# Local attention with global tokens, fused with a SoLU feed-forward: PSUM in two shared pools, q and k loaded 8 tokens a partition, and dummy products on the tensor engine

## The chip, the cores and the metric

The kernel runs on 1 core of one Trainium2 chip. The metric is device time in microseconds (us) of one execution; a time given for a kernel is the median of its runs.

## The reference

Two stages, both exact in the reference (fp32 in, fp32 out; the kernel computes its products in fp16). The first is attention for 4 batches, 8 heads, 768 tokens, 64 numbers a head. A query sees the 96 keys up to its own place and, besides, the first 8 tokens of the sequence:

```python
scores = scale * np.matmul(q, k.transpose(0, 1, 3, 2))
rel = pos[:, None] - pos[None, :]
is_global = pos[None, :] < int(n_global)
is_local = (rel >= 0) & (rel < int(n_local))
dist = np.where(is_global & ~is_local, float(n_local), np.abs(rel))
scores = np.where(is_global | is_local, scores - slopes * dist, -1000000000.0)
a = softmax(scores); x = np.matmul(a, v)
```

The second is a feed-forward layer on the 3072 rows of 512 numbers that come out (heads side by side):

```python
h = x @ w_in                                   # 3072 x 1024
solu = h * softmax(h)
ln = (solu - mean(solu)) / np.sqrt(var(solu) + 1e-06) * g_ln
out = ln @ w_out                               # 3072 x 512
```

## The kernel before

**Tiles.** The 3072 tokens are 24 tiles of 128 tokens, `n` = 0 to 23; a batch is 6 tiles. The work of a tile is a string of small tasks, and each task is one function of the kernel:

- once a batch, for each of 4 pairs of heads and for q and k (8 "pairs" a batch): `load_pair` (L243, a DMA on SP's queue), `cast_pair` (L250, fp32 to fp16, on POOL, in the first batch also on DVE), `turn_pair` (L256, 6 transposes on the tensor engine, PE, of 128 columns each, into the PSUM tile `pt`), `order_pair` (L264, a copy from PSUM on DVE or ACT that puts tokens in order);
- for each tile: `load_v` and `cast_v`; for each half of the heads `scores` (L278, 8 small products into `ps`, 4 in a batch's first tile), `score_exp` (L293, ACT), `mask_mul` (L308, DVE, multiplies by a table that holds bias and mask) and `av` (L316, 8 products of 65 columns into `pav`); `norm` (L332, DVE); `turn_x` (L343, 4 transposes) and `copy_x` (L349, DVE); `ffn_in` (L356, 8 products of 512 columns into `ph`); `ffn_exp` (L378, ACT); `ffn_u` (L383, DVE); `turn_u` (L389, a transposing DMA on SP's queue); `ffn_sq` (L393, ACT); `ffn_stats` and `ffn_pow` for the row's factor; `ffn_out` (L414, 8 products of 512 columns into `po`); `scale_out` (L423, ACT or DVE); `store` (L433, DMA on SP's queue);
- `global_k` and `global_v` (L270, L236, POOL) carry the 8 global keys and values from one tile's block to the next;
- once: `load_w_in` (L442, a DMA on POOL's queue, which also casts), `load_w_out` (L445, four DMAs on SP's queue), `gw_round`, `gw_mean` and `gw_centre` (L450 to L469), which make the second weight matrix with g and the mean folded in. `gw_mean` needs all four pieces of w_out, and every `ffn_out` needs all eight `gw_centre`.

**PSUM.** Eight banks. Before, each kind of tile has its own place: `ps` two banks, `pav` two, `ph` two, one bank for all transposes (`pt`) and one for `po`. So there is one tile of each kind at a time.

**Order.** The instructions run on each engine in the order in which they are written. `Plan` (L22) makes that order: it keeps a clock for each engine, a cost for each task, counts of free buffers (`rooms`), and a due time for each task from the table `DUE`; of the tasks that could start next it takes the one due first. The order is fixed when the program is built. SP issues DMAs in order too, each waiting for the DMA eight before it.

**Token layout.** A load puts 6 consecutive tokens of q or k on a partition (`a=NA`); a transpose handles one of the 6 for 128 partitions, and `order_pair` writes with a step of 6 elements to bring the 768 tokens into sequence.

Of the kernel before, what the change touches and what calls it, by code (L numbers as in the profile page):

```python
# [10 lines left out]
FP32 = mybir.dt.float32  # L11
# [6 lines left out]
P = 128  # L18
# [3 lines left out]
class Plan:  # L22
# [19 lines left out]
    def add(self, name, engs, emit, due, after=(), takes=(), frees=(), load=0.0):  # L42

        assert name not in self.tasks, name
        self.tasks[name] = (engs, emit, due, tuple(after), takes, frees, load,
                            len(self.tasks))

    def ready(self, task, eng):
        _, _, _, after, takes, _, load, _ = task
        t = self.free[eng]  # L50
# [13 lines left out]
    def run(self):  # L64
        log, left = [], dict(self.tasks)
        while left:
# [16 lines left out]
            engs, emit, due, after, takes, frees, load, _ = left.pop(name)  # L83
# [17 lines left out]
def kernel(  # L101
# [22 lines left out]
    NP = H // 2  # L124
    GT = 2
    T = 4.34
# [36 lines left out]
    with tc.manual_schedule():  # L163
        ident = const.tile([P, P], FP16, name="ident")
# [9 lines left out]
        nc.gpsimd.iota(diff_i, pattern=[[P, 2], [1, P]], base=0, channel_multiplier=-1)  # L174
# [24 lines left out]
        for h in range(H):  # L199
# [13 lines left out]

        gp, ve, sc = "POOL", "DVE", "ACT"
# [3 lines left out]
            rooms={"s": 1, "av": 1, "t": 1, "h": 1, "o": 1, "vst": 4, "raw": 10,  # L218
# [24 lines left out]
        def load_pair(b, w, pr):  # L243
            t = sb.tile([P, 2, NA * D], FP32, name="raw", bufs=10)
            nc.sync.dma_start(  # L245
                out=t, in_=(q, k)[w][b, 2 * pr : 2 * pr + 2].rearrange(
                    "m (p a) d -> p m (a d)", a=NA))
            raws[b, w, pr] = t

        def cast_pair(b, w, pr, eng):  # L250
            t = sb.tile([P, NA, 2, D], FP16, name="qkn", bufs=4)
# [4 lines left out]
        def turn_pair(b, w, pr):  # L256
            pt = pts[b, w, pr] = psum.tile([P, NA, P], FP16, name="pt", tag="t")
            src = qkn.pop((b, w, pr))
            for a in range(NA):
                nc.tensor.transpose(  # L260
                    out=pt[:, a, :], in_=src[:, a].rearrange("p m d -> p (m d)"),
                    identity=ident)

        def order_pair(b, w, pr, eng):  # L264
            if b not in qkT:
                qkT[b] = sb.tile([P, 2 * NP, S], FP16, name="qkT")
            dst = qkT[b][:, w * NP + pr, :].rearrange("p (t a) -> p t a", a=NA)
            ENG[eng](out=dst, in_=pts.pop((b, w, pr)).rearrange("p a t -> p t a"))  # L268
# [331 lines left out]
```

## Time and profile before

| | |
|---|---|
| runs | 170.33, 170.55, 172.1 us; median 170.55 |
| the profiled execution | 169.84 us |
| its span, first to last instruction | 168.1 us |
| busy: PE, ACT, DVE, POOL | 142.3, 127.3, 118.4, 73.8 us |
| DMA | 34.85 MB, mean 207 GB/s |

The profile is of one execution. Its span is 1.74 us shorter than that execution's own time: what lies before the first and behind the last instruction. Engines are PE (tensor engine, matrix products), PEld (its weight loads), DVE (vector), ACT (scalar), POOL (GpSimd), SP (sync); SPq is SP's queue of DMA issues. "L361" is a line of the kernel. Rows of the timeline give start, duration, engine, line, operation, output<-input, count of merged instructions, and in brackets the idle time before with what ended it. A merged row of products on PE ends some 0.16 us later than its successor begins, since products overlap; the chain of waits gives the same pieces without the overlap.

### The profile page before, as it was taken

How to read it: one execution, taken by the hardware profiler on the slowest of the kernel's cores; microseconds unless marked ns; L12 is line 12 of the kernel's file. 1: busy time of each engine (PE TensorE's matmuls, PEld its weight loads, DVE VectorE, ACT ScalarE, POOL GpSimd, SP SyncE). 2: the span in 40 equal slices, each digit the busy share in tenths (PEclk: the TensorE clock that was granted, in tenths of full speed). 3: DMA queues.
4: the chain of work that ended last, by engine and by line, in shares of the span. 5: the costliest groups of instructions: out<-in, count | busy, mean ns of one | idle time of the engine just before them, and what ended most of it. 6: DMA issues, size and time to landing. Idle time of an engine off the chain costs nothing.

```text
span 168.1 us, 3666 instructions
## 1 busy us (share of the span) xinstructions
PE 142.3 (85%) x1384; PEld 78.7 (47%) x1384; DVE 118.4 (70%) x221; ACT 127.3 (76%) x201; POOL 73.8 (44%) x154
## 2 busy tenths in 40 slices
PE   0346479878799999999999999999999999998670
PEld 0334253455465565555545455555454555543220
DVE  1355066799998968887898778987899888744300
ACT  3955585988898978999878887879787977667511
POOL 6410116576983878636775475730404133011100
PEclk9999999999999999999999999999999999999998
DMA  5999999499999999999999999834534336545841
GB/s 177 314 314 209 349 322 346 97 278 281 189 263 312 264 359 219 226 272 226 245 304 268 260 210 257 185 96 125 127 80 113 96 95 125 125 125 125 95 161 62
DMA packets 65138, 34.85 MB, mean 207 GB/s; under 512 B 52320, under 2 KB 60512, under 8 KB 65120
## 3 DMA queue, kind: packets, MB, share of 16 engines
q1 hardware_dynamic: 64592, 33.57, 81.4%
q0 software_dynamic: 528, 1.05, 3.3%
q8 instruction: 11, 0.18, 0.5%
q14 instruction: 7, 0.06, 0.1%
HBM read 23.07 MB, written 6.29 MB: 175 GB/s over the span
## 4 chain that ended last, share of the span: by engine, by line
PE 44%; DMA 26%; SPq 16%; POOL 6%; issue 4%; DVE 2%; ACT 1%; POOLq 0%; ACTq 0%
PE ph L361 16%; PE po L418 14%; DMA raw<-in_k_dram 10%; DMA vst<-in_v_dram 6%; SPq L229 6%; SPq L245 6%; PE ps L287 5%; DMA uT<-u 5%; PE pav L325 5%; DMA raw<-in_q_dram 4%; SPq L447 3%; POOL qkn L252 3%; PE pt L260 2%; PE pt L347 2%; POOL vo L234 2%
## 5 line engine op out<-in xcount | busy, mean ns | idle before, releaser
L361 PE MATMUL ph<-w_in_sb,xT 128*128 128x512 f16 x192 | 47.1, 390 | 0.9 <-DVE u L385 0.9
L418 PE MATMUL po<-gw_sb,uT 128*128 128x512 f16 x192 | 45.3, 379 | 2.7 <-ACT osb L428 1.6
L298 ACT ACTIVATE eb<-ps 128x1024 f16<-128x1024 f32 x40 | 40.7, 1018 | 1.2 <-PE ps L287 0.7
L312 DVE TENSOR_TENSOR eb<-eb,mask 128x1024 f16<-128x1024 f16 (+1 forms) x48 | 32.8, 693 | 6.1 <-ACT eb L302 4.0
L385 DVE SCALAR_TENSOR_TENSOR u<-e,ph 128x1024 f16<-128x1024 f16 x24 | 29.2, 1216 | 8.2 <-ACT e L381 6.4
L381 ACT ACTIVATE e<-ph 128x1024 f16<-128x1024 f32 x24 | 24.6, 1024 | 11.2 <-PE ph L361 11.0
L260 PE MATMUL pt<-ident,qkn 128*128 128x128 f16 x192 | 18.4, 241 | 12.7 <-DVE qkn L252 5.3
L395 ACT ACTIVATE sq<-u 128x1024 f16<-128x1024 f16 x24 | 25.4, 1059 | 4.6 <-DVE u L385 4.6
L418 PEld LDWEIGHTS <-uT 128*128 128x128 f16 x192 | 17.6, 98 | 21.5 <-issue 2.2
L252 POOL CAST qkn<-raw 128x768 f16<-128x768 f32 x25 | 21.0, 840 | 14.7 <-DMA raw<-in_q_dram 8.6
L361 PEld LDWEIGHTS <-xT 128*128 128x128 f16 x192 | 17.8, 99 | 20.5 <-issue 3.2
L234 POOL CAST vo<-vst 128x512 f16<-128x512 f32 x24 | 16.5, 691 | 19.6 <-DMA vst<-in_v_dram 19.2
L287 PE MATMUL ps<-qkT 64*128 64x128 f16 x352 | 20.4, 230 | 4.9 <-ACT eb L298 1.9
L260 PEld LDWEIGHTS <-qkn 128*128 128x128 f16 x192 | 14.0, 107 | 16.4 <-issue 7.4
L428 ACT ACTIVATE osb<-po,rs 128x512 f32<-128x512 f32 x16 | 11.0, 684 | 11.1 <-PE po L418 8.3
L268 ACT COPY qkT<-pt 128x768 f16<-128x768 f16 x19 | 15.2, 801 | 5.4 <-PE pt L260 5.2
L287 PEld LDWEIGHTS <-qkT 64*128 64x128 f16 x352 | 11.3, 98 | 16.9 <-issue 11.1
L340 DVE TENSOR_TENSOR x<-pav,rl 128x512 f16<-128x512 f32 x24 | 16.6, 691 | 0.8
L325 PE MATMUL pav<-vo,eb 128*128 128x65 f16 x352 | 16.7, 196 | 0.2 <-POOL vo L234 0.2
L268 DVE COPY qkT<-pt 128x768 f16<-128x768 f16 x13 | 12.4, 955 | 5.8 <-PE pt L260 5.8
L412 POOL TENSOR_TENSOR rs<-vs,nhalf 128x2 f32<-128x2 f32 (+1 forms) x13 | 8.9, 685 | 14.9 <-DVE vs L407 14.5
L325 PEld LDWEIGHTS <-eb 128*128 128x128 f16 x352 | 13.1, 99 | 3.1 <-issue 0.8
(48 smaller groups left out, 111.3 us busy)
## 6 DMA issues: line engine op xcount, KB each, us to landing
raw<-in_q_dram SPq DMA_DIRECT2D x16, 384.0 KB, 5.5
raw<-in_k_dram SPq DMA_DIRECT2D x16, 384.0 KB, 5.2
vst<-in_v_dram SPq DMA_DIRECT2D x24, 256.0 KB, 5.7
out_dram<-osb SPq DMA_DIRECT2D x24, 256.0 KB, 2.7
w_out<-in_moe_w_out_dram SPq DMA_DIRECT2D x4, 512.0 KB, 10.7
w_in_sb<-in_moe_w_in_dram POOLq DMA_DIRECT2D x1, 1024.0 KB, 11.7
uT<-u SPq DMA_TRANSPOSE x24, 3.7
g_sb<-in_moe_g_ln_dram SPq DMA_DIRECT2D x1, 4.0 KB, 7.8
```

Source lines behind the costliest of these rows:

```text
L252: ENG[eng](out=t.rearrange("p a m d -> p m a d"), in_=raws.pop((b, w, pr)).rearrange("p m (a d) -> p m a d", d=D))
L260: nc.tensor.transpose(out=pt[:, a, :], in_=src[:, a].rearrange("p m d -> p (m d)"), identity=ident)
L268: ENG[eng](out=dst, in_=pts.pop((b, w, pr)).rearrange("p a t -> p t a"))
L287: nc.tensor.matmul(out=ps[:, m, slot, blk, :], lhsT=qkT[b][r, NP + pr, ts(a - blk, P)], rhs=qkT[b][r, pr, ts(a, P)], start=True, stop=True)
L298: nc.scalar.activation(out=eb.rearrange("p m s b f -> p (m s b f)"), in_=ps.rearrange("p m s b f -> p (m s b f)"), func=AF.Exp, scale=inv_ ...
L312: nc.vector.tensor_tensor(out=eb.rearrange(pat), in0=eb.rearrange(pat), in1=mk.rearrange(pat if n % NA else "p m s f -> p (m s f)"), op=AL ...
L325: nc.tensor.matmul(out=pav[:, half, ds(i * (D + 1), D + 1)], lhsT=eb[:, m, slot, blk, :], rhs=vo[:, b % 2, a - blk, 4 * half + i, :], star ...
L361: nc.tensor.matmul(out=ph[:, ds(fh * 512, 512)], lhsT=xT[:, j, :], rhs=w_in_sb[:, j, ds(fh * 512, 512)], start=(j == 0), stop=(j == NCC - 1))
L381: nc.scalar.activation(out=es[n], in_=phs[n], func=AF.Exp, accum_out=acc)
L385: nc.vector.scalar_tensor_tensor(out=us[n], in0=es.pop(n), scalar=1.0, in1=phs.pop(n), op0=ALU.mult, op1=ALU.mult, accum_out=sums(n, 1))
L395: nc.scalar.activation(out=sq, in_=us[n], func=AF.Square, scale=D_FF ** -0.5, accum_out=sums(n, 2))
L418: nc.tensor.matmul(out=po, lhsT=uT[:, c, :], rhs=gw_sb[:, c, :], start=(c == 0), stop=(c == NFC - 1))
```

## The change

It has these parts.

- **PSUM.** Two pools: `big`, three places of two banks, taken by `ps`, `pav` and `ph` alike, and `one`, two places of one bank, for transposes, `po` and `pm`. A tile takes the place that came free first in the plan. `rooms` in the plan is changed to match.
- **q and k.** A load has 96 partitions with 8 consecutive tokens each (2048 bytes a row instead of 1536, 192 rows instead of 256). Eight transposes of 96 columns instead of six of 128. Keys are still put in sequence (a step of 8). Queries of a tile stay by place on the partition: place 16*a+t of a tile holds its token 8*t+a, so that the copy for q writes runs of 16 elements. The mask is built for that order, and the store writes rows back in sequence: its DRAM side is 8 x 16 rows of 512 numbers.
- **Dummy products.** 220 products of a 128 x 128 zero tile with itself into a PSUM tile `wp` that nothing reads, put by the plan at fixed times (`WARM`) among the first tiles' work. `wp` takes one place of `big` until the last of them.
- **w_in and the hold.** The plan now puts the w_in DMA on POOL behind the first v cast and the first `global_k`. The first SP load emitted after it must wait: `hold` writes one element of its buffer on POOL, behind the w_in issue.
- **The end.** The last tile's `ffn_out` is cut in two halves of 256 columns, each scaled and stored by itself.
- **Order.** A new `DUE` table, a new `T`, and changed costs in the plan, so nearly every instruction moves.

The diff, cut:

```diff
-    def add(self, name, engs, emit, due, after=(), takes=(), frees=(), load=0.0):
+    def add(self, name, engs, emit, due, after=(), takes=(), frees=(), load=0.0, at=0.0):
...
-        t = self.free[eng]
+        t = max(self.free[eng], at)
...
+    TP = 8
+    SP = S // TP
+    QP = P // TP
     GT = 2
-    T = 4.34
+    T = 5.787
     LAG = 7
...
+        warm_w = const.tile([P, P], FP16, name="warm_w")
+        nc.vector.memset(warm_w, 0.0)
...
-        nc.gpsimd.iota(diff_i, pattern=[[P, 2], [1, P]], base=0, channel_multiplier=-1)
+        nc.gpsimd.iota(diff_i, pattern=[[P, 2], [1, TP], [TP, QP]], base=0,
+                       channel_multiplier=-1)
...
-            rooms={"s": 1, "av": 1, "t": 1, "h": 1, "o": 1, "vst": 4, "raw": 10,
+            rooms={"big": 3, "one": 2, "vst": 4, "raw": RAW,
...
         def load_pair(b, w, pr):
-            t = sb.tile([P, 2, NA * D], FP32, name="raw", bufs=10)
+            t = sb.tile([SP, 2, TP * D], FP32, name="raw", bufs=RAW)
+            hold(t)
             nc.sync.dma_start(
                 out=t, in_=(q, k)[w][b, 2 * pr : 2 * pr + 2].rearrange(
-                    "m (p a) d -> p m (a d)", a=NA))
+                    "m (p a) d -> p m (a d)", a=TP))
...
-            pt = pts[b, w, pr] = psum.tile([P, NA, P], FP16, name="pt", tag="t")
+            pt = pts[b, w, pr] = psum.tile([P, TP, SP], FP16, name="pt", tag="one", bufs=2)
             src = qkn.pop((b, w, pr))
-            for a in range(NA):
+            for a in range(TP):
                 nc.tensor.transpose(
                     out=pt[:, a, :], in_=src[:, a].rearrange("p m d -> p (m d)"),
-                    identity=ident)
+                    identity=ident[0:SP, 0:SP])
...
-            dst = qkT[b][:, w * NP + pr, :].rearrange("p (t a) -> p t a", a=NA)
-            ENG[eng](out=dst, in_=pts.pop((b, w, pr)).rearrange("p a t -> p t a"))
+            dst, pt = qkT[b][:, w * NP + pr, :], pts.pop((b, w, pr))
+            if w:
+                ENG[eng](out=dst.rearrange("p (t a) -> p t a", a=TP),
+                         in_=pt.rearrange("p a t -> p t a"))
+            else:
+                ENG[eng](out=dst.rearrange("p (n a t) -> p a n t", a=TP, t=QP),
+                         in_=pt.rearrange("p a (n t) -> p a n t", t=QP))
...
-            ps = pss[n, half] = psum.tile([P, 2, 2, 2, P], FP32, name="ps", tag="s")
+            ps = pss[n, half] = psum.tile([P, 2, 2, 2, P], FP32, name="ps", tag="big", bufs=3)
...
-                pavs[n] = psum.tile([P, 2, 512], FP32, name="pav", tag="av")
+                pavs[n] = psum.tile([P, 2, 512], FP32, name="pav", tag="big", bufs=3)
...
-            ph = phs[n] = psum.tile([P, D_FF], FP32, name="ph", tag="h")
+            ph = phs[n] = psum.tile([P, D_FF], FP32, name="ph", tag="big", bufs=3)
...
+        CUT = {NT - 1: 2}
+
+        def ffn_out(n, i):
+            w = D_MODEL // CUT.get(n, 1)
+            po = pos[n, i] = psum.tile([P, w], FP32, name="po", tag="one", bufs=2)
...
-        def store(n):
-            nc.sync.dma_start(out=out[ts(n, P), :], in_=osbs.pop(n))
+        def store(n, i):
+            w = D_MODEL // CUT.get(n, 1)
+            nc.sync.dma_start(out=out[ts(n, P), ds(i * w, w)].rearrange(
+                "(t a) c -> a t c", a=TP), in_=osbs.pop((n, i)))
...
+        gate = []
+        def hold(t):
+            if gate:
+                nc.gpsimd.memset(t[0:1, 0:1, 0:1], 0.0)
+                gate.clear()
         def load_w_in():
+            gate.append(1)
             nc.gpsimd.dma_start(out=w_in_sb, in_=moe_w_in.rearrange("(j p) f -> p j f", p=P))
...
+        WARM = [0.6 + 0.107 * i for i in range(80)] + [9.2 + 0.12 * i for i in range(140)]
+        wps = []
+        def warm():
+            if not wps:
+                wps.append(psum.tile([P, P], FP32, name="wp", tag="big", bufs=3))
+            nc.tensor.matmul(out=wps[0], lhsT=warm_w, rhs=warm_w, start=True, stop=True)
...
+        for i, t in enumerate(WARM):
+            add(("wm", i), {"PE": 0.1 if i < 40 else 0.055}, lambda e: warm(), 0,
+                after=[("wm", i - 1)] if i else [], takes=() if i else ("big",),
+                frees=("big",) if i == len(WARM) - 1 else (), at=t)
```

**The order at three places.** First POOL's queue from the last cast of the first batch on. Before:

```order
L211 MEMSET meanw 128x128
L252 CAST qkn<-raw 128x2x6x64
L443 DMA w_in_sb<-in_moe_w_in_dram 128x4x1024
L234 CAST vo<-vst 128x8x64
L272 COPY qkT<-qkT 128x4x8 x2
L234 CAST vo<-vst 128x8x64 x2
L252 CAST qkn<-raw 128x2x6x64 x2
```

The same place in the changed kernel (L243 casts v, L289 is `global_k`, L247 `global_v`, L471 the hold):

```order
L218 MEMSET meanw 128x128
L262 CAST qkn<-raw 96x2x8x64 x2
L243 CAST vo<-vst 128x8x64
L289 COPY qkT<-qkT 128x4x8
L476 DMA w_in_sb<-in_moe_w_in_dram 128x4x1024
L243 CAST vo<-vst 128x8x64
L289 COPY qkT<-qkT 128x4x8
L243 CAST vo<-vst 128x8x64
L247 COPY vo<-vo 8x520
L289 COPY qkT<-qkT 128x4x8
L471 MEMSET vst 1x1
```

The w_in issue has moved behind the cast of v for tile 0 and the `global_k` of tile 1, and the hold stands behind the `global_k` of tile 3. The load that it gates is v of tile 3, the 17th DMA on SP's queue; behind it there stand all of batch 1's q and k.

Second, DVE where the second weight matrix is centred (L467 before, L501 now). Before:

```order
L385 SCALAR_TENSOR_TENSOR u,st<-e,ph 128x1024
L312 TENSOR_TENSOR eb_374<-eb_374,mask 128x1024
L467 SCALAR_TENSOR_TENSOR gw_sb<-w_out_69,g_sb,pm 128x512 x2
L336 RECIPROCAL rl<-pav 128x8
L340 TENSOR_TENSOR x_430<-pav,rl 128x512
L467 SCALAR_TENSOR_TENSOR gw_sb<-w_out_69,g_sb,pm 128x512
L312 TENSOR_TENSOR eb_434<-eb_434,mask 128x1024
L351 COPY xT<-pt 128x512
```

Now (L329 is the mask, L353 and L357 `norm`, L284 the copy of q, L368 `copy_x`, L402 `ffn_u`):

```order
L329 TENSOR_TENSOR eb_599<-eb_599,mask 128x1024
L501 SCALAR_TENSOR_TENSOR gw_sb<-w_out_69,g_sb,pm 128x512 x8
L353 RECIPROCAL rl<-pav 128x8
L357 TENSOR_TENSOR x_729<-pav,rl 128x512
L284 COPY qkT<-pt 128x8x6x16
L329 TENSOR_TENSOR eb_636<-eb_636,mask 128x1024
L368 COPY xT<-pt 128x512
L353 RECIPROCAL rl<-pav 128x8
L357 TENSOR_TENSOR x_801<-pav,rl 128x512
L402 SCALAR_TENSOR_TENSOR u,st<-e,ph 128x1024
```

All eight now stand in one block, ahead of the first `ffn_u`; before they were strewn over five tiles and the first `ffn_u` came ahead of them.

Third, the products at the end of PE's queue, one row for each group of equal products. Before:

```order
L418 MATMUL po_2500<-gw_sb_71,uT_2283 128x512
L347 MATMUL pt_2515<-ident_74,x16_2511 128x128
L361 MATMUL ph_2526<-w_in_sb_68,xT_2490 128x512
L418 MATMUL po_2544<-gw_sb_71,uT_2366 128x512
L361 MATMUL ph_2565<-w_in_sb_68,xT_2522 128x512
L418 MATMUL po_2582<-gw_sb_71,uT_2457 128x512
L418 MATMUL po_2601<-gw_sb_71,uT_2524 128x512
L418 MATMUL po_2625<-gw_sb_71,uT_2574 128x512
L418 MATMUL po_2637<-gw_sb_71,uT_2612 128x512
```

Now:

```order
L438 MATMUL po_2784<-gw_sb_71,uT_2631 128x512
L364 MATMUL pt_2803<-ident_76,x16_2795 128x128
L378 MATMUL ph_2810<-w_in_sb_68,xT_2760 128x512
L378 MATMUL ph_2826<-w_in_sb_68,xT_2819 128x512
L438 MATMUL po_2848<-gw_sb_71,uT_2679 128x512
L438 MATMUL po_2866<-gw_sb_71,uT_2797 128x512
L438 MATMUL po_2890<-gw_sb_71,uT_2821 128x512
L438 MATMUL po_2910<-gw_sb_71,uT_2860 128x512
L438 MATMUL po_2922<-gw_sb_71,uT_2883 128x256
L438 MATMUL po_2936<-gw_sb_71,uT_2883 128x256
```

The last two `ph` stand side by side, and five tiles' `po` come behind the last `ph` instead of four, the fifth in halves.

More of the change, by code (lines that the diff above doesn't have):

```diff
@@ L82, in run @@
             at, name = best[2:]
-            engs, emit, due, after, takes, frees, load, _ = left.pop(name)
+            engs, emit, due, after, takes, frees, load, _, _ = left.pop(name)
             _, eng, t, us = min((x[0] + x[4], e, x[0], x[4])
@@ L535 @@
             add(("u", n), {ve: 1.26}, lambda e, n=n: ffn_u(n), n,
-                after=[("he", n)], takes=("u", "ut"), frees=("h", "e"))
+                after=[("he", n)], takes=("u", "ut"), frees=("big", "e"))
             add(("ut", n), {"SP": 0.5}, lambda e, n=n: turn_u(n), n, after=[("u", n)],
@@ L545 @@
                 add(("pw", g), {gp: 0.7}, lambda e, g=g: ffn_pow(g), n, after=[("st", g)])
[L546 to L552 removed]
+            cut = CUT.get(n, 1)
+            for i in range(cut):
+                x = (n, i)
+                add(("o", *x), {"PE": 1.75 / cut}, lambda e, x=x: ffn_out(*x), n,
+                    after=[("ut", n)] + [("gc", j) for j in range(NFC)]
+                    + ([("o", n, i - 1)] if i else []),
+                    takes=("one",), frees=("uT",) if i == cut - 1 else ())
+                add(("os", *x), {sc: 0.2 + 0.5 / cut, ve: 0.2 + 0.55 / cut},
+                    lambda e, x=x: scale_out(*x, e), n, after=[("o", *x), ("pw", g)],
+                    takes=("osb",), frees=("one",))
+                add(("w", *x), {"SP": 0.5}, lambda e, x=x: store(*x), n,
+                    after=[("os", *x)], frees=("osb",), load=0.75 / cut)
         add("w_in", {gp: 1.2}, lambda e: load_w_in(), 0, load=5.4)
```

78 lines of the change are left out of this document (37 added, 41 removed), and 22 rows, old and new, of the table DUE.

## The prediction

> **What bounds the kernel now.** I read the busy time by stretches first. Columns: stretch, its length, busy time and count for PE, PEld, DVE, ACT, POOL, then granted clock, DMA share, GB/s.
>
> ```profile
> 0.00:10.00 10.00, 2.17 (x18) 1.84 (x19) 3.54 (x7) 6.12 (x18) 5.70 (x21) 1.00 0.81 268
> 10.00:20.00 10.00, 5.50 (x49) 3.77 (x47) 3.66 (x6) 5.52 (x7) 0.61 (x1) 1.00 1.13 264
> 20.00:30.00 10.00, 8.18 (x64) 4.24 (x65) 5.93 (x11) 6.93 (x10) 3.46 (x6) 1.00 1.08 333
> ...
> 110.00:120.00 10.00, 10.00 (x103) 5.50 (x103) 8.09 (x16) 7.90 (x13) 2.00 (x7) 1.00 0.37 97
> ```
>
> ```profile
> 30.00:60.00 30.00, 26.56 (x319) 16.42 (x317) 27.71 (x52) 27.16 (x41) 21.43 (x37) 1.00 1.00 247
> 60.00:150.00 90.00, 89.38 (x898) 48.21 (x897) 73.80 (x135) 74.08 (x115) 41.54 (x88) 1.00 0.82 185
> 150.00:168.10 18.10, 10.54 (x46) 4.21 (x44) 3.74 (x12) 7.47 (x13) 1.10 (x2) 0.96 0.51 119
> ```
>
> There are three stages with three limits. Up to 30 us PE idles for 14 us of 30 while the DMA engines are full: the loads bind. From 30 to 60 DVE is busy 27.71 of 30 and PE idles 3.4: DVE is fullest there. From 60 to 150 PE works 89.38 of 90: PE alone binds, and only fewer products could shorten it. Behind 150 PE idles 7.6 of 18.1. So the change can win at both ends, hardly in the middle.
>
> Next, PE's rows in order of time, and, from the chain of waits, what a group costs where PE is full.
>
> ```profile
> 4.44 0.82 PE L260 MATMUL pt<-ident,qkn 128*128 128x128 f16 x6 [4.44 <-DVE qkn L252]
> ...
> 24.93 3.60 PE L361 MATMUL ph<-w_in_sb,xT 128*128 128x512 f16 x8
> ...
> 29.44 2.28 PE L463 MATMUL pm<-gw_sb,meanw 128*128 128x512 f16 x8
> ...
> 37.10 1.90 PE L361 MATMUL ph<-w_in_sb,xT 128*128 128x512 f16 x8
> ...
> 52.35 1.89 PE L361 MATMUL ph<-w_in_sb,xT 128*128 128x512 f16 x8
> ```
>
> ```profile
> 59.27 1.73 PE ph L361 x8
> 61.00 0.22 PE pt L347 x4
> 61.22 0.33 PE ps L287 x8
> ...
> 62.23 1.73 PE po L418 x8
> ...
> 69.52 0.44 PE pt L260 x6
> ...
> 130.66 0.59 PE pav L325 x16
> ```
>
> The first `ph` takes 3.60 us, the later ones 1.90: PE runs at half speed until about 30 us, though the granted clock reads 1.00 throughout. The product at 52.35 is the fifth `ph`. I use it as a mark: ahead of it both orders hold nearly the same products (17 pairs turned, 104 score products, four `ph`, one `po`; 92 products of `pav` before and 88 now, 5 and 6 `turn_x`). What is behind it can be compared as a sum.
>
> Last, the end, from the timeline:
>
> ```profile
> 151.99 1.89 PE L361 MATMUL ph<-w_in_sb,xT 128*128 128x512 f16 x8 [0.74 <-DVE u L385]
> ...
> 153.92 1.02 ACT L381 ACTIVATE e<-ph 128x1024 f16<-128x1024 f32 x1 [0.79 <-PE ph L361]
> ...
> 155.06 1.22 DVE L385 SCALAR_TENSOR_TENSOR u<-e,ph 128x1024 f16<-128x1024 f16 x1 [1.75 <-ACT e L381]
> ...
> 156.84 2.63 SPq L391 DMA_TRANSPOSE uT<-u  x1
> ...
> 162.12 1.90 PE L418 MATMUL po<-gw_sb,uT 128*128 128x512 f16 x8 [1.14 <-DMA uT<-u]
> ...
> 164.20 0.69 ACT L428 ACTIVATE osb<-po,rs 128x512 f32<-128x512 f32 x1 [2.44 <-PE po L418]
> ```
>
> The last `ph` ends at about 153.7 (151.99 + 1.73). From there a chain of 14.4 us, exp, u, transposing DMA, `po`, scaling, store, runs to 168.1.
>
> **The change part by part.** The sum is made for the span; the profiled execution took 169.84 for a span of 168.1, and the median of the runs, 170.55, is 0.7 above it.
>
> *The front, to the fifth `ph`.* Rows for it:
>
> ```profile
> L312 DVE TENSOR_TENSOR eb<-eb,mask 128x1024 f16<-128x1024 f16 x40 | 29.2, 733 | 2.1 <-ACT eb L298 1.8
> L340 DVE TENSOR_TENSOR x<-pav,rl 128x512 f16<-128x512 f32 x24 | 16.6, 691 | 0.8
> L268 DVE COPY qkT<-pt 128x768 f16<-128x768 f16 x13 | 12.4, 955 | 5.8 <-PE pt L260 5.8
> L351 DVE COPY xT<-pt 128x512 f16<-128x512 f16 x24 | 10.1, 421 | 5.6 <-PE pt L347 5.4
> L467 DVE SCALAR_TENSOR_TENSOR gw_sb<-w_out,g_sb,pm 128x512 f16<-128x512 f32 x8 | 5.8, 738 | 0.0
> L336 DVE RECIPROCAL rl<-pav 128x8 f32<-128x8 f32 x24 | 4.9, 203 | 2.1 <-PE pav L325 1.7
> L312 DVE TENSOR_TENSOR eb<-eb,mask 128x512 f16<-128x512 f16 x8 | 3.9, 490 | 4.0 <-ACT eb L302 4.0
> L385 DVE SCALAR_TENSOR_TENSOR u<-e,ph 128x1024 f16<-128x1024 f16 x24 | 29.2, 1216 | 8.2 <-ACT e L381 6.4 <-DMA uT<-u 1.5
> ```
>
> When do the weights come? SP's queue carries 8 loads of 0.39 MB, three of v (0.79 MB) and w_out (2.1 MB) ahead of the gated one: 6.0 MB. At the pace of the first three rows (2.7 MB by 10, 5.3 by 20, then 0.33 a us) that is 22 us, a little more once w_in joins. Add rounding on ACT and the mean product, 1.73 on a fast PE instead of 2.28: it ends at about 26 instead of 31.7 (29.44 + 2.28). Then DVE's new row is fixed: eight centrings, 8 x 0.738 = 5.9; up to the `norm` of tile 5, which the fifth `ph` stands behind, four `norm` (0.894 each, 3.6), four masks (2.9) and a short one (0.5), three `copy_x` (1.3), three `ffn_u` (3.6) and four copies of q. Such a copy isn't in the trace. As 768 elements with a step it is 0.955; as 512 in runs 0.421. In runs, 768 would be 0.42 to 0.63; I take 0.55, and keep 0.955 as the upper bound: 2.2 (or 3.8). Sum 14.1, so 26 + 5.9 + 14.1 = 46.0, then `turn_x` and scores, 0.55: 46.6. With waits like those from 30 to 60 (2.3 of 30), 1.5 more: 48. The lower bound takes off the overlap of neighbours (their rows overlap by about 0.07 each, 22 operations, 1.5): 45. The upper is no gain at all: 52.35. I take **47.5**, near the DVE rows.
>
> What could be later than DVE there: w_in, POOL's casts, and the exps.
>
> ```profile
> 8.12 1.09 POOL L443 DMA_DIRECT2D w_in_sb<-in_moe_w_in_dram  x1
> ...
> 21.60 0.21 POOL L272 COPY qkT<-qkT 128x32 f16<-128x32 f16 x1 [1.94 <-ACT eb L302]
> ```
>
> ```profile
> DMA to landing us min/median/max: 11.7/11.7/11.7
> ```
>
> ```profile
> L252 POOL CAST qkn<-raw 128x768 f16<-128x768 f32 x25 | 21.0, 840 | 14.7 <-DMA raw<-in_q_dram 8.6 <-DMA raw<-in_k_dram 5.0 <-PE po L418 1.0
> ```
>
> w_in was issued at 8.12 and landed 11.7 later (the row of its tile, above), at 20, beside the other loads. Now it waits for the first `global_k`, at 21.60 before. That should come at 17 to 19, since batch 0's pairs no longer queue for one transpose bank at half speed. With less beside it I expect it landed at 27 to 29. The first `ffn_u` is due on DVE at about 36 (26 + 5.9, two `norm`, q copy, mask, two `copy_x`), so w_in is covered by DVE; that cover is gone if it lands after 32 (`ph` 1.73 and exp 1.02 ahead of `ffn_u`). POOL's eight casts of batch 1, 0.84 x 1024/768 = 1.12 each, 9 us and some 4 of v work from about 28: done at 41, ahead of tile 6's scores.
>
> *PSUM, `big`.* `ph` no longer waits for the `ffn_u` of the tile before, and two transposes or `po` can stand at once. From 60 to 150 this is worth nothing, since PE idles 0.62 there; at the end it lets the last two `ph` stand together. It costs a wait if `ph` and `pav` hold their places long: `ph` 1.73 + 1.02 + 1.22 with hops 4.3, `pav` about 2.2, two `ps` of 1.5, together 9.5 a tile of three places x 5.2.
>
> *Layout.* Eight turns of 96 columns for six of 128. PE's chain shows 0.44 or 0.33 for six (0.055 a product) and 0.037 for one of 65 columns (0.59 over 16). 96 columns lie between: 0.33 to 0.44 for eight. I take +0.04 a pair, 15 pairs behind the mark: **+0.6** (0 to 1.7). Casts of 1024 elements and DVE's copies are hidden behind PE from 60 on, where DVE has 16 us idle of 90. The other masks cost the same operations on POOL, under the first load's flight.
>
> *Dummies.* 220 x 0.055 = 12 us of PE, up to 30 us, where PE idled 14 us and real work at half speed, 15.86 busy, gives back some 7. I charge nothing: what they delay (a transposition by a run of up to 18, 1 us) is hidden by the loads.
>
> [...]
>
> *From the mark to the last `ph`.* Before, 52.35 to 153.7, 101.4 us, of which the rows' products make 97.8 (15 pairs 5.4, 248 score products 10.3, 260 of `pav` 10.4, 19 `turn_x` 4.2, 20 `ph` 34.6, 19 `po` 32.9) and 3.6 waits and jitter. Now one `po` fewer lies ahead of the last `ph`: 97.8 - 1.7 = 96.1, + 0.6, + waits. The gap of 0.74 before the last `ph` and its like go, others stay: **2.6** (1.6 to 5).
>
> *The end.* Counted from the last `ph`'s end: exp, u and the issue come at +2.8 (before 3.1). The transpose landed 5.2 after issue; SP's queue now has both last transposes ahead of the last stores, so I take 4.5: +7.3. Meanwhile PE has four `po`, 6.9, so it hardly idles. Two half `po` 1.8, scaling 0.2 + 0.45, store 3.2 as before (168.1 - 164.9): **13.0** (12.2 to 14), against 14.4.
>
> **Sum**: 47.5 + 96.1 + 0.6 + 2.6 + 13.0 = 159.8 of span, + 1.74 = 161.5 beside the 169.84; on the median's footing (+0.7) **162**. Ends: 45 + 96.1 + 0 + 1.6 + 12.2 + 2.4 = 157.3 and 52.35 + 96.1 + 1.7 + 5 + 14 + 2.4 = 171.6.
>
> **The rivals.** *A, the front gains nothing.* DVE and ACT were 92% busy from 30 to 60 and their work is about the same; the new block of eight centrings holds up `ffn_u`. Against it: the block starts 5 us earlier. Then the mark stays at 52.35: 162 + 4.9 = **167**.
>
> *B, the stores hold up the loads.* The store's DRAM side is now 8 x 16 rows. If its 128 rows go out on 8 DMA engines instead of 16, those 8 carry, a tile, (0.52 + 0.26 + 0.26)/16 + 0.26/8 MB instead of 1.31/16, a fifth more. DMA is full (1.00 to 1.2) while loads last and 0.37 when they have ended, at 110 us. A fifth more on 80 us of loads would end them at about 125, late for the last tiles; I price it at 4 us of PE waits: **166**. Against it: DMA fell to 0.37 from 110 on, so the loads had ended long before the last tiles needed them. [...]
>
> *C, slower: the hold.* w_in and batch 1's loads now hang on `global_k` of tiles 1 and 3, hence on ACT's exps, which stand behind roundings that wait for w_out. If the order doesn't bring `global_k` forward, w_in is issued at 21.8 and lands at 34.6, and batch 1's first load is issued at about 32 instead of 20.60:
>
> ```profile
> 20.60 3.52 SPq L245 DMA_DIRECT2D raw<-in_q_dram  x1
> ```
>
> Eleven us later puts the mark at about 60, and the time at 162 + 12.5 = **174.5**. It decides once the mark comes later than 56, that is when the hold opens after 28 us.
>
> *D, PE stays at half speed in spite of the dummies.* Zeros might not count as work. Then 220 x 0.11 = 24 us of dummies fill the front, and the mark comes near 60 as well: **174**.
>
> **How the numbers follow.** Forecast 0.62, A 0.15, B 0.12, C 0.08, D 0.03. The range reaches from the forecast's lower end to above A and B: 157.5 to 168.5. About 1% is what a measurement of this kernel can tell from no change. Faster by over 1% (below 168.8): forecast, B and most of A, 0.86. Slower by over 1%: C, D less what is milder, 0.09. Same: 0.05.
>
> **What would show it.** Right: `ph` of 1.73 from the first on; the first `ph` at 27 to 30 and the fifth at 46 to 49; PE above 97% from there to the last `ph`, at about 146; then 13 us. A would show in the fifth `ph` after 51, B in PE waits for v or raw or in stores that land later than 2.7 us, C in the gated v load issued after 28, D in transposes of 0.8 us at 15 us. The forecast is wrong if PE idles more than 3 us between the fifth and the last `ph`.

## The result and the profile after

The changed kernel takes **181.01 us** (median of 4, 179.36 to 183.72) beside 170.67 for the kernel before (170.33 to 172.1): ratio 1.056, 95% interval 1.044 to 1.067. Predicted were 162.0 and a range of 157.5 to 168.5, so the sign was wrong. Ratios here leave out runs over 1.5% above the fastest of the same kernel, as the profiled one of these four is (183.72 us, mean granted clock 0.912 where the others had 0.949 to 0.964), so the terms read from it are together about 3 us too large.

The same stretches as before (length, busy time and count of PE, PEld, DVE, ACT, POOL, then granted clock, DMA share, GB/s), now of the changed kernel:

```profile
0.00:10.00 10.00, 8.43 (x102) 7.82 (x102) 4.77 (x8) 6.19 (x18) 3.95 (x19) 1.00 0.85 202
10.00:20.00 10.00, 6.99 (x88) 6.22 (x89) 4.43 (x7) 3.06 (x5) 2.63 (x3) 0.68 1.09 287
20.00:30.00 10.00, 9.89 (x160) 8.31 (x159) 6.79 (x14) 8.10 (x11) 4.01 (x7) 0.81 0.93 183
110.00:120.00 10.00, 10.00 (x105) 5.54 (x104) 9.20 (x17) 7.84 (x12) 7.30 (x14) 1.00 1.16 216
```

```profile
30.00:60.00 30.00, 25.70 (x280) 15.75 (x278) 23.07 (x42) 18.23 (x28) 16.89 (x26) 0.89 1.19 219
60.00:150.00 90.00, 84.40 (x861) 47.60 (x860) 70.02 (x122) 66.99 (x103) 48.51 (x92) 0.94 1.01 196
```

The last two columns tell most. In the first 10 us, when pair loads are in flight, the DMA engines are as busy as before (0.85 for 0.81) and bring 202 GB/s for 268; from 10 to 20 us, with w_out and v among the loads, it is 287 for 264. At 110 us, where the share was 0.37 because the loads had ended, it is 1.16. The page's queue row has the same 33.57 MB as before in a larger part of a longer span, 91.8% of 181.9 us for 81.4% of 168.1 (167 us of packet time for 137). The row now, and before:

```profile
q1 hardware_dynamic: 62488, 33.57, 91.8%
...
q1 hardware_dynamic: 64592, 33.57, 81.4%
```

The marks of the prediction, from PE's timeline:

```profile
34.70 3.62 PE L378 MATMUL ph<-w_in_sb,xT 128*128 128x512 f16 x16
45.49 2.95 PE L378 MATMUL ph<-w_in_sb,xT 128*128 128x512 f16 x8
52.34 1.89 PE L378 MATMUL ph<-w_in_sb,xT 128*128 128x512 f16 x8
58.86 1.90 PE L378 MATMUL ph<-w_in_sb,xT 128*128 128x512 f16 x8
...
162.78 3.62 PE L378 MATMUL ph<-w_in_sb,xT 128*128 128x512 f16 x16
```

The row at 34.70 holds two `ph`, so the row at 58.86 begins with the fifth. The last two end at 166.2 (162.78 + 2 x 1.73). So the three terms of the sum are 58.9, 107.4 and 15.7, where 47.5, 99.3 (96.1 + 0.6 + 2.6) and 13.0 were predicted: all three are missed, by 11.4, 8.1 and 2.7.

How a late load reaches PE shows best at 69 us. POOL's and PE's timelines there:

```profile
64.64 0.96 POOL L243 CAST vo<-vst 128x512 f16<-128x512 f32 x1
70.88 1.04 POOL L262 CAST qkn<-raw 96x1024 f16<-96x1024 f32 x1 [5.28 <-DMA raw<-in_k_dram]
71.86 0.61 POOL L247 COPY vo<-vo 8x520 f16<-8x520 f16 x1
72.42 0.20 POOL L289 COPY qkT<-qkT 128x32 f16<-128x32 f16 x1
```

```profile
69.05 0.23 PE L304 MATMUL ps<-qkT 64*128 64x128 f16 x2
72.68 0.50 PE L304 MATMUL ps<-qkT 64*128 64x128 f16 x6 [3.39 <-POOL qkT L289]
73.11 3.60 PE L378 MATMUL ph<-w_in_sb,xT 128*128 128x512 f16 x8
```

A cast waits 5.28 us for its load. Behind it on POOL stands `global_k` (L289), a copy of 0.2 us for which the scores of the running tile wait, and PE idles 3.39. Then the next `ph` takes 3.60 instead of 1.90: PE has fallen back to half speed; in the page's row of the granted clock (40 slices of 4.55 us, tenths) the slice from 72.8 us on, the 17th, reads 5:

```profile
PEclk9995589995799998589999969999999999999995
```

The granted clock is 0.77 on average from 71 to 72 us and 0.50 from 72 on, so it fell some 2.3 us into this gap of 3.39. It also fell to 0.50 at 13.5 and at 41 us, where no gap was longer than 1.2 us; PE had been busy for 1.3 us of the 3 from 10 to 13, and of the 3 from 38 to 41.

### The profile page after: what moved, and what is told of

Its sections match the earlier page's. It is cut to its first block, busy times and chain, and to the rows that moved or that the text cites. A ratio compares the mean times of both kernels' runs of the same rounds, so it can differ in the third digit from the quotient of the medians.

```text
span 181.9 us, 4265 instructions
## 1 busy us (share of the span) xinstructions
PE 160.6 (88%) x1676; PEld 99.0 (54%) x1676; DVE 125.8 (69%) x230; ACT 120.9 (66%) x193; POOL 81.1 (45%) x156
## 3 DMA queue, kind: packets, MB, share of 16 engines
q1 hardware_dynamic: 62488, 33.57, 91.8%
q0 software_dynamic: 528, 1.05, 3.5%
## 4 chain that ended last, share of the span: by engine, by line
PE 47%; DMA 29%; POOL 7%; issue 4%; SPq 4%; DVE 4%; ACT 1%; POOLq 0%; ACTq 0%
DMA raw<-in_k_dram 18%; PE ph L378 17%; PE po L438 12%; DMA vst<-in_v_dram 6%; PE ps L304 6%; PE pav L342 5%; POOL qkn L262 4%; PE pt L270 3%; PE wp L513 3%; DMA out_dram<-osb 3%; DMA raw<-in_q_dram 2%; SPq L255 2%; PE pt L364 2%; SPq L408 1%; POOL vo L247 1%
## 5 line engine op out<-in xcount | busy, mean ns | idle before, releaser
L315 ACT ACTIVATE eb<-ps 128x1024 f16<-128x1024 f32 x40 | 40.9, 1022 | 13.7 <-PE ps L304 13.3
L378 PE MATMUL ph<-w_in_sb,xT 128*128 128x512 f16 x192 | 49.5, 407 | 0.0
L438 PE MATMUL po<-gw_sb,uT 128*128 128x512 f16 (+1 forms) x200 | 44.9, 371 | 1.0 <-ACT osb L450 1.0
L329 DVE TENSOR_TENSOR eb<-eb,mask 128x1024 f16<-128x1024 f16 (+1 forms) x48 | 36.2, 764 | 9.4 <-ACT eb L315 8.6
L262 POOL CAST qkn<-raw 96x1024 f16<-96x1024 f32 x26 | 27.6, 1062 | 33.2 <-DMA raw<-in_k_dram 24.5
L402 DVE SCALAR_TENSOR_TENSOR u<-e,ph 128x1024 f16<-128x1024 f16 x24 | 29.1, 1211 | 1.7 <-ACT e L398 1.6
L270 PE MATMUL pt<-ident,qkn 96*128 96x96 f16 x256 | 18.8, 227 | 8.1 <-POOL qkn L262 5.7
L270 PEld LDWEIGHTS <-qkn 96*128 96x128 f16 x256 | 15.3, 109 | 14.9 <-POOL qkn L262 8.9
L450 ACT ACTIVATE osb<-po,rs 128x512 f32<-128x512 f32 (+1 forms) x18 | 11.9, 663 | 15.5 <-PE po L438 7.1
L243 POOL CAST vo<-vst 128x512 f16<-128x512 f32 x24 | 16.8, 702 | 11.6 <-DMA vst<-in_v_dram 11.5
L513 PE MATMUL wp<-warm_w 128*128 128x128 f16 x220 | 20.6, 259 | 1.0 <-DVE warm_w L168 1.0
L513 PEld LDWEIGHTS <-warm_w 128*128 128x128 f16 x220 | 17.2, 119 | 1.9 <-DVE warm_w L168 1.0
L357 DVE TENSOR_TENSOR x<-pav,rl 128x512 f16<-128x512 f32 x24 | 16.6, 692 | 0.8
L247 POOL COPY vo<-vo 8x520 f16<-8x520 f16 x16 | 9.7, 609 | 14.2 <-PE pav L342 14.2
```

Source lines behind the costliest of these rows:

```text
L262: ENG[eng](out=t.rearrange("p a m d -> p m a d"), in_=raws.pop((b, w, pr)).rearrange("p m (a d) -> p m a d", d=D))
L270: nc.tensor.transpose(out=pt[:, a, :], in_=src[:, a].rearrange("p m d -> p (m d)"), identity=ident[0:SP, 0:SP])
L315: nc.scalar.activation(out=eb.rearrange("p m s b f -> p (m s b f)"), in_=ps.rearrange("p m s b f -> p (m s b f)"), func=AF.Exp, scale=inv_ ...
L329: nc.vector.tensor_tensor(out=eb.rearrange(pat), in0=eb.rearrange(pat), in1=mk.rearrange(pat if n % NA else "p m s f -> p (m s f)"), op=AL ...
L378: nc.tensor.matmul(out=ph[:, ds(fh * 512, 512)], lhsT=xT[:, j, :], rhs=w_in_sb[:, j, ds(fh * 512, 512)], start=(j == 0), stop=(j == NCC - 1))
L402: nc.vector.scalar_tensor_tensor(out=us[n], in0=es.pop(n), scalar=1.0, in1=phs.pop(n), op0=ALU.mult, op1=ALU.mult, accum_out=sums(n, 1))
```

## The experiments

Three causes could be read from this trace: the layout (theory L: loads on 96 partitions are slow), the store by place (S), and the hold with the late w_in (H, the prediction's rival C). H had all its signs: w_in issued at 24.33, the gate opened by POOL at 30.13, the mark at 58.9.

```profile
24.33 0.95 POOL L476 DMA_DIRECT2D w_in_sb<-in_moe_w_in_dram  x1 [0.33 <-issue]
...
30.13 0.09 POOL L471 MEMSET vst<- 1x1 f32 x1
```

All variants of the changed kernel keep the planner's costs and so the same order of work; only what is emitted differs. The runs were made on several chips, so ratios, each to the kernel before on the same chip, are safer than differences of medians.

**The old layout put back**, with the mask patterns of before and all the rest of the change (the diff, cut; the mask patterns are left out):

```diff
-    TP = 8
+    TP = 6
...
-            if w:
-                ENG[eng](out=dst.rearrange("p (t a) -> p t a", a=TP), ...
-            else:
-                ENG[eng](out=dst.rearrange("p (n a t) -> p a n t", a=TP, t=QP), ...
+            ENG[eng](out=dst.rearrange("p (t a) -> p t a", a=TP),
+                     in_=pt.rearrange("p a t -> p t a"))
...
-            nc.sync.dma_start(out=out[ts(n, P), ds(i * w, w)].rearrange(
-                "(t a) c -> a t c", a=TP), in_=osbs.pop((n, i)))
+            nc.sync.dma_start(out=out[ts(n, P), ds(i * w, w)], in_=osbs.pop((n, i)))
```

> The changed kernel with only the old q, k layout put back: 128 partitions of 6 tokens, six turns, queries in sequence, the old mask patterns, and the store by row. Pools, order, hold, w_in and dummies stay as changed. Theory L (a load on 96 partitions moves at 202/268 = 0.75 of the pace, so 12.6 MB of q and k cost 62 us of full DMA instead of 47): most of the loss goes, 163 to 168 us, fifth ph at 47 to 51, first 10 us near 268 GB/s. Theory S (only the store by place is slow): also 163 to 168, told apart by the run with the row store alone. Theory H (the hold and the late w_in): stays at 175 to 180, since batch 1's loads still wait until about 30 us.

Measured: **160.66 us** (160.33 to 160.95), before 169.7, ratio 0.948 (0.944 to 0.952). H is out: the hold and the late w_in are still there. This version beats both kernels. Its marks, from PE's timeline, and its stretches:

```profile
29.64 3.61 PE L370 MATMUL ph<-w_in_sb,xT 128*128 128x512 f16 x16
37.66 1.89 PE L370 MATMUL ph<-w_in_sb,xT 128*128 128x512 f16 x8
43.58 1.89 PE L370 MATMUL ph<-w_in_sb,xT 128*128 128x512 f16 x8
48.83 1.90 PE L370 MATMUL ph<-w_in_sb,xT 128*128 128x512 f16 x8
...
142.41 3.62 PE L370 MATMUL ph<-w_in_sb,xT 128*128 128x512 f16 x16
```

```profile
0.00:10.00 10.00, 7.93 (x106) 7.60 (x106) 4.28 (x9) 6.12 (x18) 4.66 (x20) 1.00 0.82 249
...
60.00:110.00 50.00, 49.94 (x530) 28.96 (x529) 44.46 (x77) 41.83 (x66) 31.73 (x64) 1.00 1.18 258
110.00:150.00 40.00, 40.00 (x360) 21.26 (x359) 31.14 (x65) 32.08 (x52) 10.75 (x26) 1.00 0.54 115
```

The mark is at 48.83, from there to the last `ph`'s end (145.9) it is 97.0, and the end 12.6 of a span of 158.5. PE is full from 60 on (89.94 of the 90 us to 150), and the granted clock reads 1.00 up to 150 us and 0.97 behind. These are the prediction's terms.

**The layout alone in the kernel before**: `raw` as 96 x (2 x 512), eight turns, both q and k copied into sequence, row store.

> The kernel before with the 96-partition layout of q and k alone: 8 tokens a partition, eight turns of 96 columns, both q and k brought into sequence as before, row store, old pools, old order, no hold, no dummies. Theory L: first 10 us near 202 GB/s, batch 0's last pair cast at about 18 instead of 13, 177 to 182 us. Theories S and H: 170 to 172 us, as before, since neither the store nor the hold is in it.

Measured: 180.53 (179.37 to 182.1), ratio 1.063 (1.057 to 1.069): 10.8 us of loss without any other part of the change. L holds. Median time to landing of a q load (the last number) is 7.1 us here and 5.5 before:

```profile
raw<-in_q_dram SPq DMA_DIRECT2D x16, 384.0 KB, 7.1
...
raw<-in_q_dram SPq DMA_DIRECT2D x16, 384.0 KB, 5.5
```

**Queries in sequence and the row store, loads still on 96 partitions.** The edit is that of the first run without its first line.

> The changed kernel with queries copied into sequence (as k is) and stores by row; the 96-partition loads stay. Theory S (the 8x16-row store goes out on half the DMA engines and takes the loads' time): 170 to 174 us, store issue back to 0.42 us, the end 2 us shorter. Theory L: 178 to 181; DVE's q copies cost 0.95 instead of 0.56, which is hidden. Theory H: 178 to 181 as well.

Measured: 174.08 (172.18 to 174.75), ratio 1.024 (1.016 to 1.031). So L and S both hold: between 1.056 and 1.024 lies the store together with the order of the queries, 3.2% of 170, or 5.5 us (6.9 by the medians); between 1.024 and 0.948 the layout, 7.6%, or 13 us. A later run changes the store alone.

```profile
58.65 1.90 PE L370 MATMUL ph<-w_in_sb,xT 128*128 128x512 f16 x8
...
156.84 3.62 PE L370 MATMUL ph<-w_in_sb,xT 128*128 128x512 f16 x16
```

By terms: 58.7, 101.7 and 12.7 of a span of 173.0. By these traces the store had cost nothing ahead of the mark, 5.7 behind it and 3.0 at the end; that is more than 5.5 together, since the changed kernel's terms are read too large. The layout costs 9.8 ahead of the mark and 4.7 behind.

**The change without the hold**: the line `gate.append(1)` taken out.

> The changed kernel with the gate never set, so that no load waits for POOL's memset behind w_in; w_in itself still stands at its late place on POOL. Theory H: batch 1's first load is issued at 21 instead of 30.7, the fifth ph comes at 48 to 52 and the time is 168 to 172 us. Theory L: the DMA engines stay full to about 125 us whatever the order of the loads; w_in shares the pace with batch 1's loads and lands later; 177 to 182 us.

Measured: 181.94 (179.52 to 183.17), ratio 1.069 (1.060 to 1.078). The fifth `ph` came at 61.19, later than with the hold.

**The transfers by themselves.** One kernel that only moves data, each group held back until the one before has landed.

> Only DMAs, nothing of the reference is computed: six phases, each held back until the one before has landed. Ten pair loads of 0.39 MB as 128 partitions x 6 tokens; ten as 96 partitions (0 to 95) x 8 tokens; ten as 96 partitions that alternate between 0 to 95 and 32 to 127; six as 64 partitions x 12 tokens; then eight stores of 0.26 MB by row, eight in the order of 8 x 16 rows, eight in the order of 16 x 8 rows. Theory Partitions (the pace goes with the partitions written): from 13 us for the first ten, 17.5 for the 96, about 13 to 15 for the alternating ones, and 16 for the six on 64 (8 if the partitions didn't matter). Rival Packets (the size of a piece matters: 1.5, 2 and 3 KB): 13, 12, 12 and 7. Stores: if 8 outer rows mean 8 DMA engines, the 8 x 16 phase takes twice the time of the phase by row, and the 16 x 8 phase the same as by row; if it is only the scattered rows, 8 x 16 and 16 x 8 are alike.

POOL copies one column of each tile as it lands, so the starts of these copies are the landings. Four forms, with the source of each in its last name (`full` 128 x 6 tokens, `low` 96 x 8, `mix` 96 at alternating places, `half` 64 x 12):

```profile
10.30 0.17 POOL L43 COPY acc<-full 32x1 f32<-32x1 f32 x1 [0.88 <-DMA full<-in_q_dram]
...
13.46 0.17 POOL L43 COPY acc<-full 32x1 f32<-32x1 f32 x1 [0.88 <-DMA full<-in_k_dram]
...
23.99 0.17 POOL L43 COPY acc<-low 32x1 f32<-32x1 f32 x1 [1.32 <-DMA low<-in_k_dram]
...
28.34 0.18 POOL L43 COPY acc<-low 32x1 f32<-32x1 f32 x1 [1.27 <-DMA low<-in_q_dram]
...
41.11 0.18 POOL L43 COPY acc<-mix 32x1 f32<-32x1 f32 x1 [1.43 <-DMA mix<-in_k_dram]
...
47.23 0.17 POOL L43 COPY acc<-mix 32x1 f32<-32x1 f32 x1 [1.47 <-DMA mix<-in_k_dram]
...
56.02 0.17 POOL L43 COPY acc<-half 32x1 f32<-32x1 f32 x1 [1.83 <-DMA half<-in_k_dram]
...
61.60 0.17 POOL L43 COPY acc<-half 32x1 f32<-32x1 f32 x1 [1.67 <-DMA half<-in_q_dram]
```

The same 0.39 MB lands every 1.05 us on 128 partitions (3.16 over 3), every 1.45 on 96 (4.35 over 3), every 1.86 on 64 (5.58 over 3): 374, 271 and 211 GB/s. Alternating between the lower and the upper 96 partitions gains nothing: 1.53 (6.12 over 4); why it doesn't is not shown. The rival of the pieces, which wanted the larger pieces to be no slower, is out. For the stores, three groups of eight follow; the wait of POOL's next memset is the time until all have landed:

```profile
64.05 4.51 SPq L74 DMA_DIRECT2D out_dram<-osb  x8
71.27 0.53 POOL L75 MEMSET osb<- 128x512 f32 x1 [7.24 <-DMA out_dram<-osb]
71.83 9.04 SPq L77 DMA_DIRECT2D out_dram<-osb  x8
86.31 0.52 POOL L78 MEMSET osb<- 128x512 f32 x1 [14.51 <-DMA out_dram<-osb]
86.86 6.16 SPq L80 DMA_DIRECT2D out_dram<-osb  x8
```

Eight row stores take 7.2 us, eight in the order 8 x 16 take 14.5: twice. The page's row of the DMA engines' busy share (40 slices of 2.4 us) reads 5 in that stretch, slices 32 to 35, but 9 under the row stores, slices 28 and 29, and mostly 9 while the loads run, for `low` as for `full`:

```profile
DMA  1999951999998199999808999519913555515992
```

Eight in the order 16 x 8 were done by the end of the span, 9.9 us with the program's own end in it. So it is the outer 8, not the scattering. The issue of the 8 x 16 stores on SP also takes twice the time (9.04 us for 4.51), but it is over at 80.9, 5 us ahead of the last landing, so here the issue isn't the bound. In the changed kernel the median issue of a store takes 0.62 us, and 0.42 in the kernel before, with its row store; what share that has in the store's 5 us is not separated.

**Partitions or pieces.**

> Only DMAs, nothing of the reference is computed: six phases of eight loads each, one phase after the other. In the run before, successive loads of 0.39 MB landed 1.05 us apart on 128 partitions in pieces of 1.5 KB, 1.45 apart on 96 in pieces of 2 KB, 1.85 on 64 in pieces of 3 KB: either the partitions or the pieces do it. Phases here: 128 x 2 pieces of 1.5 KB (0.39 MB); 128 x 1 of 2 KB (0.26 MB); 128 x 2 of 2 KB (0.52 MB); 96 x 2 of 1.5 KB (0.29 MB); 96 x 2 of 1 KB (0.20 MB); 128 x 2 of 1 KB (0.26 MB). Theory Partitions (128 take 374 GB/s, 96 about 271): 1.05, 0.70, 1.40, 1.09, 0.73, 0.70 us apart. Rival Pieces (2 KB pieces cost 121 ns of a DMA engine, 1.5 KB 66 ns): 1.05, 0.97, 1.94, 0.79, about 0.53 and 0.70.

From the third landing of each group to the eighth, five intervals:

| Form | KB a partition | MB | us apart | 0.35 us per KB |
|---|---|---|---|---|
| 128 x 2 x 1.5 KB | 3 | 0.39 | 1.05 (7.62 to 12.85) | 1.05 |
| 128 x 1 x 2 KB | 2 | 0.26 | 0.74 (17.70 to 21.42) | 0.70 |
| 128 x 2 x 2 KB | 4 | 0.52 | 1.42 (28.84 to 35.95) | 1.40 |
| 96 x 2 x 1.5 KB | 3 | 0.29 | 0.97 (42.68 to 47.52) | 1.05 |
| 96 x 2 x 1 KB | 2 | 0.20 | 0.67 (52.16 to 55.52) | 0.70 |
| 128 x 2 x 1 KB | 2 | 0.26 | 0.71 (61.80 to 65.33) | 0.70 |

Pieces of 2 KB are not slow on 128 partitions. Here the time goes with how much each partition gets: 0.35 us per KB to within 8%, whether 96 or 128 partitions take part. (On 64 partitions, in the run before, it was 0.31: 1.86 us for 6 KB.) Why it does is not shown. A pair of heads on 96 partitions is 4 KB a partition instead of 3.

**Fewer bytes on 96 partitions.** Is it the loads alone, or also eight turns and longer casts?

```diff
-            t = sb.tile([SP, 2, TP * D], FP32, name="raw", bufs=RAW)
+            t = sb.tile([SP, 2, 6 * D], FP32, name="raw", bufs=RAW)
...
-                    "m (p a) d -> p m (a d)", a=TP))
+                    "m (p a) d -> p m (a d)", a=TP)[:, :, 0 : 6 * D])
...
+            ENG[eng](out=dst[:, :, 0:6], in_=raw)
+            ENG[eng](out=dst[:, :, 6:8], in_=raw[:, :, 0:2])
```

> The kernel on 96 partitions with queries in sequence and the store by row (174.08 us), which loads only 6 of each partition's 8 tokens of q and k (0.29 MB a pair instead of 0.39; tokens 6 and 7 are copied from 0 and 1, so a quarter of q and k is left out). Casts in two pieces of 768 and 256 elements, eight turns of 96 and all copies stay. If the pace of the loads makes the 13.4 us between this layout and the old one (160.66): a load is now about as long as one on 128 partitions (0.97 to 1.09 us alone against 1.05), so most goes: 161 to 165 us. If turns, casts and copies of the layout make them: 171 to 175.

Measured: 163.7 (160.97 to 163.84), before 170.44. Of the 13.4 us between the medians 174.08 and 160.66, 10.4 are gone with the fourth KB by the median, and between 10.2 and 13.1 by the single runs (163.84, 163.78, 163.62 and 160.97). So the loads make most of it. What the rest is, turns, a second cast or the spread of these runs, stays open.

**The store by place on the good layout** (the first run, with the store's order put back to 8 x 16 rows):

> The changed kernel with the old q, k layout (160.66 us), but with the store in the order of 8 x 16 rows (the rows of a tile then leave in another order than the reference's). Theory: the store by place is worth 6 to 8 us only where the DMA engines are already the bound; here they end the loads by 115, so a part shows: 2 us at the end (12.6 to 15) and 1 to 4 in the middle, 163 to 167. Rival (the loss between the two runs on 96 partitions came from DVE's and ACT's changed copies): 160 to 161.

Measured: 166.71 (165.24 to 170.5), ratio 0.977 (0.967 to 0.986) beside 0.948: about 5 us, 6.0 by the medians. This is the store alone, so the copies of the queries, the rival, are out. Terms: mark 49.15, then 100.8, then 15.7. The end's 3.1 are as in the changed kernel; the middle loses 3.8.

**The dummies** (the first run without them):

> The changed kernel with the old q, k layout (160.66 us) and none of the 220 dummy products. If they do what the prediction took from them (full speed for the real products ahead of 30 us): first ph of 16 products takes 7 us instead of 3.6, the fifth ph comes 2 to 5 us later, 163 to 166. If they only fill idle time: 160 to 161, with the fifth ph still at 49.

Measured: 163.51 (162.14 to 163.83), ratio 0.958 (0.949 to 0.966) beside 0.948 (0.944 to 0.952): 1.7 us by the ratios, whose intervals overlap, 2.9 by the medians. In the profiled execution, the longest of the four, the terms are mark 52.07, then 96.8, then 13.2: nearly all in the front.

```profile
29.28 3.61 PE L370 MATMUL ph<-w_in_sb,xT 128*128 128x512 f16 x16 [0.44 <-ACT eb L307]
37.85 1.89 PE L370 MATMUL ph<-w_in_sb,xT 128*128 128x512 f16 x8
45.34 3.37 PE L370 MATMUL ph<-w_in_sb,xT 128*128 128x512 f16 x8
52.07 1.90 PE L370 MATMUL ph<-w_in_sb,xT 128*128 128x512 f16 x8
```

Without dummies PE does work at half speed up to 27 us (six turns take 0.82 us for 0.50, the mean product 3.59 for 1.89), but the first `ph` come as early and as fast as with them. The loss comes later. The row at 45.34 stood at 43.58 with dummies, 1.8 us earlier, and its 3.37 us add 1.5. Ahead of it, at 41.4, PE waits 1.32 us for DVE's `u`, where it waits 0.36 with dummies. Whether the missing dummies bring this about, or the chance of one execution, is not shown, and with the dummies their place in `big` is gone as well.

**The hold and w_in on the good layout.** The gate never set:

> The changed kernel with the old q, k layout (160.66 us) and the gate never set. If the hold costs (batch 1's loads wait for POOL): batch 1's first load at about 21, 157 to 160. If it only gives the pace to w_in: 160 to 163, w_in lands later.

Measured: 163.25 (161.23 to 164.73), ratio 0.949 (0.939 to 0.959), beside 160.66 and 0.948 with the hold: no difference by the ratio. Two of the four runs (164.61 and 164.73) are longer than any with the hold, so a small gain from it isn't excluded. And w_in issued as POOL's first instruction, without the gate:

> The changed kernel with the old q, k layout (160.66 us), no gate, and w_in issued as POOL's first instruction instead of at 18.7 us. If w_in's late place costs: the first ph, at 29.6 with w_in landed at 28.0, comes earlier, 156 to 160. If it is right to let batch 0 and w_out go first (DMA is full from 3 us on): batch 0's pairs land 3 to 4 us later, the fifth ph at 50 to 53, 162 to 166.

Measured: 168.61 (167.7 to 169.02), ratio 0.989 (0.982 to 0.997) beside the 0.949: 7 us lost. The first `ph` came at 35.65 and the fifth at 57.83. With w_in in flight from 1.2 to 13.7 us the first piece of w_out is issued at 13.6 instead of 7.2, the last pair of batch 0 is turned at 21.8 instead of 15.2, and the mean product begins at 30.8 instead of 24.8: the front comes 6 us later as a whole. The late place is right; no run shows a gain from the hold behind it.

## Why the prediction was wrong

**The step that failed is the layout**, "+0.6 (0 to 1.7)". It counted turns, casts and copies and gave the loads no price. Those it counted came out as said: the POOL cast took 1.06 (predicted 1.12) and DVE's copy of q in runs 0.56 (0.55).

```profile
L262 POOL CAST qkn<-raw 96x1024 f16<-96x1024 f32 x26 | 27.6, 1062 | 33.2 <-DMA raw<-in_k_dram 24.5 <-DMA raw<-in_q_dram 8.5
L284 DVE COPY qkT<-pt 128x768 f16<-128x768 f16 x13 | 7.2, 556 | 5.9 <-PE pt L270 5.2 <-POOL vo L243 0.5
```

But the first of these rows also shows 33 us of waits for loads, where it was 14.7 before. The step took "the pace of the first three rows (2.7 MB by 10, 5.3 by 20, then 0.33 a us)" from loads on 128 partitions and used it for loads on 96. By the loads alone, 32 pairs x (1.45 - 1.05) is 12.8 us of more work for DMA engines that the same rows showed to be full; measured were 10.8 in the kernel before and about 13 here. Though the text said that up to 30 us "the loads bind", the edit to the loads was costed only on the engines.

**The store** was the second: "store 3.2 as before" in the end, which lost 3.1 by it. Rival B had the factor right (twice the time: 14.5 us for 7.2) and a price of 4 us for the 5 to 7 measured. That a store goes out on 8 engines, the term of its sum, no run shows; the runs showed the mean busy share of all 16 at 0.5 under the 8 x 16 stores and at 0.9 or more under the row stores, which fits it. Its condition, however, was no matter of chance: the outer 8 stood in the diff. It should have been a term of the sum, end included, and not a rival.

**The other terms held**, as the version with the old layout shows: mark 48.8 (47.5 predicted), 97.0 from there (98.7 without the layout's 0.6), end 12.6 (13.0); 160.66 us for 161.4. That the total is so close is partly luck: the mark is 1.3 late, and the stretch behind it 1.7 short. PSUM as two pools, the new order and the cut last tile were not run one by one; taken together with the dummies they did what was said of them. This also puts **rival A** out: the front gains, once the loads are as before.

**The dummies** were charged nothing and given no gain of their own; by themselves they are worth 1.7 to 2.9 us. In the one execution profiled without them the mark is at 52.07, and before it was at 52.35, so there the front's gain is gone; but it went by a wait for DVE of 1.32 us and a `ph` of 3.37 behind 41 us, not by slow products ahead of the first `ph`, which is what the dummies were for.

**Rival C** "decides once the mark comes later than 56, that is when the hold opens after 28 us". Both came true, at 58.9 and 30.1, the time was even longer than its 174.5, and it was still not the cause: with no hold at all the time was 181.94. On the old layout the same gate opened 5 us earlier:

```profile
25.06 0.09 POOL L462 MEMSET vst<- 1x1 f32 x1
```

So its lateness was an effect of the slow loads. **Rival D** had its signs too: its mark ("near 60") and its "transposes of 0.8 us at 15 us":

```profile
12.47 0.51 PE L270 MATMUL pt<-ident,qkn 96*128 96x96 f16 x8 [0.60 <-ACT qkT L280]
...
14.11 0.82 PE L270 MATMUL pt<-ident,qkn 96*128 96x96 f16 x8 [0.45 <-DVE qkn L262]
```

The granted clock was 0.50 from 13.5 to 23.7 us, in the middle of the dummies, and again near 41 and 72. But the row at 12.47 is at full speed beside the same dummies. In the first run, with the old layout, the clock stays at 1.00 up to 150 us, and the first pair is turned at 5.04, behind 42 dummies and nothing else, in 0.50 us; without dummies it takes 0.82. So zeros do count as work, though 42 of them were not always enough: in the changed kernel, in that without the hold and in the run with the early w_in the first pair still took 0.82 to 0.85 us, and the second 0.50 or 0.51. Half speed came with the waits for slow loads, and is a part of what the layout cost. How large a part is not separated.

## What to carry to other kernels

Price a load by what one partition gets, not by its bytes: 0.35 us per KB a partition here, so that the same bytes on three quarters of the partitions need about four thirds of the time (1.45 us for 1.05). When a layout changes, cost its transfers first, above all where the profile's DMA row is full, and look for the outermost size on the DRAM side. A rival's signs in the trace don't prove it (C and D had all of theirs): undo its part alone.

## What the runs showed of the hardware

- DMA engines that read as fully busy (a share of 0.9 or more) moved 271 GB/s in one form and 374 in another: the busy share doesn't tell pace.
- A store whose DRAM side has an outermost size of 8 took twice the time (14.5 for 7.2 us for eight), at a busy share of 0.5.
- Alternating the place of 96 partitions between neighbours in the queue didn't balance anything (1.53 us apart, against 1.45).
- After 3.39 us without products PE needed 3.60 us for a `ph` of 1.90, in the middle of the kernel. The granted clock fell to 0.50 behind shorter gaps too: ahead of 13.5 and of 41 us none was over 1.2 us, and PE was busy 1.3 us of 3.
- Products of zeros count as work: in the first run, with the old layout, the first pair is turned in 0.50 us behind 42 of them, without them in 0.82. In three of the eight executions profiled with them the first pair took 0.82 to 0.85, and the second 0.50 or 0.51.
